# Summing a gradient over prompts on GpSimd in place of identity matmuls, with seven rotating PSUM banks

## The chip, the cores and the metric
The kernel runs on one core of one Trainium2 chip. The metric is the device time of one execution in microseconds. PE is the matrix engine (PEld its weight loads), DVE the vector engine, ACT the scalar engine, POOL the GpSimd engine, SP the engine whose queue issues many of the transfers. DVE, ACT and PE work with PSUM, the accumulator memory of eight banks; a bank holds 128 x 512 fp32 values.

## The reference
The forward pass is a speech encoder with a joint network; the kernel computes the output and all gradients (inputs bf16):

```python
B, T, D, K = 2, 16000, 256, 3      # U = 8 prompts
...
h = gelu(conv(x, w1))[:, ::2, :]   # 3 taps, every second step kept
f = gelu(conv(h, w2))[:, ::2, :]   # 4000 steps are left
fe = jnp.einsum("btd,de->bte", f, w_f)
ge = jnp.einsum("bud,de->bue", g, w_g)
j = jnp.tanh(fe[:, :, None, :] + ge[:, None, :, :])
return jnp.einsum("btud,dv->btuv", j, w_o)
```

`reference` returns this output and the gradients of `x`, `w1`, `w2`, `g`, `w_f`, `w_g` and `w_o` for a given `grad_out` of shape 2 x 4000 x 8 x 256. On the way back the gradient of the tanh's argument, (1 - j²) · (grad_out w_oᵀ), is summed over the eight prompts to give the gradient of `fe`. That sum is what the change is about. In the code it is kept with the opposite sign (NGZ, NGFE).

## The kernel before, in words
The 4000 steps of each of the two batches are cut into chunks of 512 (the last has 416): G = 16 chunks, numbered from 0. Channels lie on the partitions: a tile of 2 x 512 columns holds 256 channels of one chunk, and W is the chunk's width.

The main loop goes over chunks n, and in each over four pairs of prompts (`joint_units`, a generator that yields after each piece of work). For each prompt u of a pair, `gj` squares the tanh on ACT (JSQ), multiplies the transposed `grad_out` by w_oᵀ on PE into a PSUM tile (L518), and on DVE forms NGZ = (JSQ - 1) · that tile (L520), one tile half at a time. Then come the output blocks (`o_block`: PE L574, copied by ACT to OUT, L576), the sum over prompts (`ngfe_acc`), and the products for w_o's gradient (`gwo`, L621) of the pair before, for which the tanh is transposed by DMA (JR, L548). At the end of a pair its outputs are stored from POOL's queue (L605).

Into this main work a second stream is woven, `fill`: after each main unit `weave` takes 0.85 units of it on the average. For a chunk n in the middle it holds, in this order: `d1_units(n - 1)` (gradient through w_f; PE L334 reads NGFE, DVE writes GF, L336), `conv_units(n + 1)` (first convolution of the next chunk, four PSUM tiles, PE L241), `d5_units(n - 1)` (GH, L366), six units of `gw2_units(n - 1)` (PE transposes copied out by DVE, L374 and L376), `conv2_units(n + 1)` (L274), the rest of `gw2_units` (sums added up by DVE, L317), and `e_units(n - 1)` (gradients of x and w1: L467, L489), with `fe_units(n + 1)` (L297) among them. What is left of `fill` after the fourth pair runs then.

The gelu and its derivative are not instructions of these units: `gelu` puts ten operations a tile (nine on DVE, a sigmoid on ACT; their line is L191, where they are called) into a list `later`, of which `pump(2)` takes two before each fill step; `conv2_units` and `fe_units` empty it first. All work on bf16 tiles of 128 x 1024 in SBUF.

PSUM: a pool `psp` of five rotating banks for all short-lived tiles (`ps`, `pst`), one bank for `GWO_ps`, and `psn` for `NGps`, a tile of 128 x 2 x 512 fp32, which fills two. NGZ has three buffers, OUT and JSQ two, X5 four.

`load_x5` loads the rows of x for w1's gradient from POOL's queue, pinned to the program order. `d1_units` calls it when its first unit is taken. POOL further stores OUT and GX and copies halo columns of HT, G1, GF and GH (L232, L256, L328, L354).

Of the kernel before, what the change touches and what calls it, by code (L numbers as in the profile page):

```python
# [14 lines left out]
FP32 = mybir.dt.float32  # L15
ALU = mybir.AluOpType
# [5 lines left out]
P = 128  # L22
KT = 2
# [3 lines left out]
U = 8  # L27
CW = 512
# [3 lines left out]
def kernel(  # L32
# [22 lines left out]
    nc = tc.nc  # L55
# [7 lines left out]
    def geom(n):  # L63
        b, ci = chunks[n]
        c0 = ci * CW
        return b, ci, c0, min(CW, MQ - c0)

    def blocks(w):
        return [(o, min(P, w - o)) for o in range(0, w, P)]
# [7 lines left out]
    ftp = pool("ftp", 2)  # L77
    fep = pool("fep", 2)
    ngp = pool("ngp", 1)
    gfp = pool("gfp", 2)  # L80
    ghp = pool("ghp", 2)
    rowp = pool("rowp", 6)
# [7 lines left out]
    jrp = pool("jrp", 2)  # L90
    outp = pool("outp", 2)
    PS = bass.MemoryType.PSUM
    psp = pool("psp", 5, space=PS)
    psn = pool("psn", 1, space=PS)
    psw = pool("psw", 1, space=PS)

    def ps_f32():
# [6 lines left out]
    ident = const.tile([P, P], BF16, name="ident")  # L104
# [52 lines left out]
    def window(n):  # L157
        b, ci, c0, W = geom(n)
        lo = c0 - 1 if ci > 0 else 0
        hi = c0 + W if ci == NCH - 1 else c0 + W - 1  # L160
        return lo, hi

    def load_x5(n, o, M):
        pin = tc.keep_in_program_order
        b = chunks[n][0]
        q0 = window(n)[0] + o
        t = x5p.tile([P, 5, D], BF16, name="X5")
        if q0 == 0:
            nc.vector.memset(t[0:1, 0, :], 0.0)
            pin(nc.gpsimd.dma_start(out=t[0:1, 1:5, :], in_=x[b, 0:4, :].rearrange("(o f) d -> o f d", o=1)))  # L170
            src = x[b, 3:4, :]
            ap5 = bass.AP(tensor=src.tensor, offset=src.offset, ap=[[4 * D, M - 1], [1, 5 * D]])
            pin(nc.gpsimd.dma_start(out=t[1:M].rearrange("p f d -> p (f d)"), in_=ap5))
        else:
            src = x[b, 4 * q0 - 1:4 * q0, :]
            ap5 = bass.AP(tensor=src.tensor, offset=src.offset, ap=[[4 * D, M], [1, 5 * D]])
            pin(nc.gpsimd.dma_start(out=t[:M].rearrange("p f d -> p (f d)"), in_=ap5))
        S[n]["X5", o] = t
# [140 lines left out]
    def d1_units(n):  # L319
        b, ci, c0, W = geom(n)  # L320
        st = S[n]
        lo, hi = window(n)
        for (o, M) in blocks(hi - lo):
            load_x5(n, o, M)
        GF = gfp.tile([P, KT, CW + 4], BF16, name="GF")
        st["GF"] = GF
        if ci > 0:
            nc.gpsimd.tensor_copy(out=GF[:, :, 1:2], in_=S[n - 1]["GF"][:, :, CW + 1:CW + 2])  # L328
        if ci == NCH - 1:
            nc.gpsimd.memset(GF[:, :, 2 + W:3 + W], 0.0)  # L330
        for mt in range(KT):
            ps = ps_f32()
            for kt in range(KT):
                nc.tensor.matmul(ps[:, :W], lhsT=WFT[:, kt, mt * P:(mt + 1) * P], rhs=st["NGFE"][:, kt, :W],  # L334
                                 start=(kt == 0), stop=(kt == KT - 1))
            nc.vector.scalar_tensor_tensor(out=GF[:, mt, 2:2 + W], in0=st["G2"][:, mt, :W], scalar=-1.0,  # L336
                                           in1=ps[:, :W], op0=ALU.mult, op1=ALU.mult)
            yield
# [184 lines left out]
            yield  # L523

    def ngfe_acc(n, u):
        W = geom(n)[3]
        st = S[n]
        if u == 0:
            st["NGps"] = psn.tile([P, KT, CW], FP32, name="NGps")
        for mt in range(KT):  # L530
            nc.tensor.matmul(st["NGps"][:, mt, :W], lhsT=ident[:], rhs=st["NGZ", u][:, mt, :W],  # L531
                             start=(u == 0), stop=(u == U - 1))
        if u == U - 1:
            st["NGFE"] = ngp.tile([P, KT, CW], BF16, name="NGFE")
            nc.scalar.copy(out=st["NGFE"][:, :, :W], in_=st["NGps"][:, :, :W])

    def load_jr(n, up):

# [16 lines left out]
    def joint_units(n, up):  # L555
        b, ci, c0, W = geom(n)
        st = S[n]
        bl = blocks(W)
        us = (2 * up, 2 * up + 1)
        for u in us:  # L560
            yield from gj(n, u)
        if n == 0:
            for k in range(len(bl)):
                jr_block(n, up, k)
                yield
        OUT = outp.tile([P, 4, 2 * V], BF16, name="OUT")
        JR = st["JR", up]

        def o_block(k):
            o, M = bl[k]  # L570
            ps = ps_f32()
            for j, u in enumerate(us):
                for kt in range(KT):
                    nc.tensor.matmul(ps[:M, j * V:(j + 1) * V], lhsT=st["JT", u][:, kt, o:o + M], rhs=WO[:, kt, :],  # L574
                                     start=(kt == 0), stop=(kt == KT - 1))
            nc.scalar.copy(out=OUT[:M, k, :], in_=ps[:M, :])  # L576

        pend = prev_gwo[0]
        o_block(0)
        yield  # L580
        o_block(1)
        if len(bl) > W // P:
            jr_block(n, up, len(bl) - 1)
        yield
        ngfe_acc(n, us[0])
        if pend is not None:
            gwo(*pend, 0)
        yield
        if pend is not None:
            gwo(*pend, 1)  # L590
        yield
        for k in range(2, len(bl)):
            o_block(k)
            yield
            if pend is not None:
                gwo(*pend, k)
        ngfe_acc(n, us[1])
        yield
        if pend is not None:
            for k in range(len(bl), len(blocks(geom(pend[0])[3]))):  # L600
                gwo(*pend, k)
        yield
        prev_gwo[0] = (n, up)
        nfull = W // P
        nc.gpsimd.dma_start(out=out_0[b, c0:c0 + nfull * P, us[0]:us[1] + 1, :].rearrange("(tb p) u v -> p tb (u v)", p=P),  # L605
                            in_=OUT[:, 0:nfull, :])
        if W > nfull * P:
            nc.gpsimd.dma_start(out=out_0[b, c0 + nfull * P:c0 + W, us[0]:us[1] + 1, :].rearrange("t u v -> t (u v)"),
                                in_=OUT[:W - nfull * P, nfull, :])
# [3 lines left out]
    def gwo(n, up, k):  # L613
        bl = blocks(geom(n)[3])
        if k >= len(bl):
            return
        o, M = bl[k]
        JR, GO = S[n]["JR", up], S[n]["GO", up]
        for j in range(2):
            for dt in range(KT):  # L620
                nc.tensor.matmul(GWO_ps[:, dt, :], lhsT=JR[:M, k, j, dt, :], rhs=GO[:M, k, j * V:(j + 1) * V],  # L621
                                 start=(n_gwo[0] == 0), stop=(n_gwo[0] == last_gwo))
                n_gwo[0] += 1


    def chain(*gens):
        for gen in gens:
            yield from gen
# [81 lines left out]
    for n in range(G):  # L710
        back, fwd = n > 0, n + 1 < G
        parts = []
        if back:
            d1, d5, gw2, e = d1_units(n - 1), d5_units(n - 1), gw2_units(n - 1), e_units(n - 1)
        if back:
            parts.append(d1)
        if fwd:
            parts.append(conv_units(n + 1))
        if back:
            parts += [d5, islice(gw2, 6)]  # L720
        if fwd:
            parts.append(conv2_units(n + 1))
        if back:
            parts += [gw2, islice(e, 5)]
        if fwd:
            parts.append(fe_units(n + 1))
        if back:
            parts.append(e)
        fill = chain(*parts)
        ratio = (0.85 if n > 0 else 0.2) if n + 1 < G else 0.72  # L730
        for up in range(U // 2):
            step = n * (U // 2) + up
            for i in range(2):
                if 2 * step + 4 + i < len(order):
                    load_got(*order[2 * step + 4 + i])
            if step + 1 < len(orderp):
                load_go(*orderp[step + 1])
            if up == 2 and n + 2 < G:
                load_x(n + 2)
            main = joint_units(n, up)  # L740
            weave(main, fill, ratio)
            if up == U // 2 - 1:
                for _ in fill:
                    pump(2)
                pump(len(later))
            for i in range(2):
                if 2 * step + 2 + i < len(order):
                    tanh(*order[2 * step + 2 + i])
            if step + 1 < len(orderp):
                load_jr(*orderp[step + 1])  # L750
    n = G - 1
    for k in range(len(blocks(geom(n)[3]))):
        gwo(*prev_gwo[0], k)
    for _ in chain(d1_units(n), d5_units(n), gw2_units(n), e_units(n)):
        pass

# [72 lines left out]
```

## Time and profile before
| what | value |
|---|---|
| median of 3 runs | 951.14 us (947.83 to 953.77) |
| the profiled execution | 953.21 us, its span 951.4 us |
| granted PE clock, mean | 0.989 |
| DMA queues' packets, share of 16 engines | 64.3% (hardware), 25.2% (software) |
| NGZ on DVE (L520) | 256 instructions, mean 668 ns |
| NGFE copy on ACT (L535) | 16 instructions, median 1000 ns |

Busy times count each engine's own instructions. A wait in square brackets in a timeline is idle time of the engine just before the instruction, with what ended it. The chain of waits runs back from the last instruction, at each step to what released it. Matmuls overlap in the array, so that each one's record is longer than the time after which the next begins.

### The profile page before, as it was taken

What the parts mean: (1) busy time and instruction counts of PE and PEld (TensorE: products, weight loads), DVE (VectorE), ACT (ScalarE), POOL (GpSimd) and SP (SyncE); (2) the same over time, 40 slices, a digit from 0 to 9 for tenths busy, and PEclk for the clock granted to TensorE, in tenths of its full rate; (3) what the DMA queues carried; (4) which work ended last, traced back from release to release, by engine and by line L of the source; (5) the groups of instructions that cost most, each with busy time, mean ns of one, the idle gap of its engine ahead of it and who ended that gap; (6) DMA issues with size and microseconds to landing.
All of it is one profiled execution on the core that took longest, in us unless ns stands there. A gap on an engine that the chain in (4) does not pass through costs nothing.

```text
span 951.4 us, 18311 instructions
## 1 busy us (share of the span) xinstructions
PE 914.8 (96%) x6976; PEld 629.1 (66%) x6976; DVE 633.1 (67%) x1364; ACT 614.4 (65%) x972; POOL 144.8 (15%) x279
## 2 busy tenths in 40 slices
PE   7889998999999999999999999899999999999997
PEld 3455665767667576766756667576676757677775
DVE  5887847678494866748587494865939578494634
ACT  2878484765848567583865848568484866858433
POOL 1002121121111112021111202012021120202121
PEclk9989999999999999999999999999999999999999
DMA  9769999799998999898799999989989997897742
GB/s 189 175 125 221 194 207 204 198 230 186 212 196 206 206 203 244 183 219 187 156 211 192 200 206 209 198 190 221 205 208 228 188 226 179 191 215 183 198 132 87
DMA packets 381816, 185.69 MB, mean 195 GB/s; under 512 B 329904, under 2 KB 365512, under 8 KB 381728
## 3 DMA queue, kind: packets, MB, share of 16 engines
q1 hardware_dynamic: 362016, 114.35, 64.3%
q0 software_dynamic: 19712, 70.18, 25.2%
q8 instruction: 54, 0.88, 0.4%
q14 instruction: 34, 0.28, 0.1%
HBM read 54.43 MB, written 50.34 MB: 110 GB/s over the span
## 4 chain that ended last, share of the span: by engine, by line
PE 53%; DVE 24%; ACT 17%; DMA 4%; issue 2%; POOL 0%; SPq 0%; ACTq 0%; POOLq 0%; DVEq 0%
PE ps L489 8%; PE ps L467 7%; PE ps L574 7%; PE GWO_ps L621 6%; DVE g_sq L191 6%; DVE g_s L191 5%; ACT JT L307 5%; PE ps L518 5%; PE pst L374 5%; PE ps L274 4%; DVE NGZ L520 4%; DVE GH L366 4%; DMA JR<-JT 3%; ACT OUT L576 3%; PE NGps L531 2%; ACT JSQ L512 2%
## 5 line engine op out<-in xcount | busy, mean ns | idle before, releaser
L520 DVE SCALAR_TENSOR_TENSOR NGZ<-JSQ,ps 128x512 bf16<-128x512 bf16 (+1 forms) x256 | 167.7, 668 | 108.1 <-PE ps L518 102.9
L576 ACT CAST OUT<-ps 128x512 bf16<-128x512 f32 (+1 forms) x256 | 150.4, 591 | 81.7 <-PE ps L574 80.1
L307 ACT ACTIVATE JT<-FE,GE 128x512 bf16<-128x512 f32 (+1 forms) x256 | 172.8, 717 | 2.6 <-PE ps L574 2.0
L512 ACT ACTIVATE JSQ<-JT 128x1024 bf16<-128x1024 bf16 (+1 forms) x128 | 133.0, 1040 | 54.5 <-DVE NGZ L520 54.0
L621 PE MATMUL GWO_ps<-GO,JR 128*128 128x256 bf16 (+1 forms) x1024 | 153.1, 273 | 9.2 <-DMA JR<-JT 9.1
L574 PE MATMUL ps<-WO,JT 128*128 128x256 bf16 (+1 forms) x1024 | 156.0, 275 | 0.1
L518 PE MATMUL ps<-GOT,WOT 128*128 128x512 bf16 (+1 forms) x512 | 138.4, 374 | 6.3 <-DVE NGZ L520 5.9
L621 PEld LDWEIGHTS <-JR 128*128 128x128 bf16 (+1 forms) x1024 | 98.7, 97 | 50.2 <-DMA JR<-JT 14.0
L574 PEld LDWEIGHTS <-JT 128*128 128x128 bf16 (+1 forms) x1024 | 98.3, 99 | 32.1 <-issue 6.2
L317 DVE TENSOR_TENSOR ACC<-ACC,ps 128x512 f32<-128x512 f32 x90 | 61.4, 684 | 83.9 <-PE ps L489 80.4
L191 ACT ACTIVATE g_s<-g_s 128x1024 bf16<-128x1024 bf16 (+2 forms) x49 | 49.2, 1004 | 89.5 <-DVE g_s L191 89.5
L467 PE MATMUL ps<-W1T,GH 128*128 128x256 bf16 (+2 forms) x768 | 103.7, 272 | 0.0
L489 PE MATMUL ps<-rows,X 128*128 128x256 bf16 (+2 forms) x768 | 93.6, 272 | 0.0
L470 ACT CAST GX<-ps 128x512 bf16<-128x512 f32 (+2 forms) x128 | 75.3, 588 | 28.3 <-PE ps L467 19.4
L241 PE MATMUL ps<-XC,W 128*128 128x512 bf16 (+1 forms) x384 | 91.0, 374 | 0.7 <-DVE JR L376 0.5
L467 PEld LDWEIGHTS <-GH 128*128 128x128 bf16 (+2 forms) x768 | 74.7, 99 | 20.6 <-issue 1.6
L605 POOL DMA_DIRECT2D out_dram<-OUT x64 | 49.1, 767 | 247.5 <-ACT OUT L576 244.1
L376 DVE COPY rows<-pst 128x1024 bf16<-128x1024 bf16 (+5 forms) x134 | 85.8, 655 | 1.4 <-PE pst L374 1.4
L479 POOL DMA_DIRECT2D out_dram<-GX x64 | 35.3, 552 | 321.1 <-ACT GX L470 315.7
L489 PEld LDWEIGHTS <-X 128*128 128x128 bf16 (+2 forms) x768 | 73.7, 97 | 14.8 <-issue 3.0
L531 PE MATMUL NGps<-NGZ,ident 128*128 128x512 bf16 (+1 forms) x256 | 80.3, 374 | 0.1
L191 DVE TENSOR_TENSOR g_sq<-g_x 128x1024 bf16<-128x1024 bf16 (+2 forms) x49 | 32.1, 655 | 68.1 <-ACT g_x L244 39.3
(122 smaller groups left out, 1156.7 us busy)
## 6 DMA issues: line engine op xcount, KB each, us to landing
GO<-in_grad_out_dram SPq DMA_DIRECT2D x56, 512.0 KB, 4.2
out_dram<-OUT POOLq DMA_DIRECT2D x56, 512.0 KB, 4.8
X<-in_x_dram POOLq DMA_DIRECT2D x58, 320.0 KB, 7.6
out_dram<-GX POOLq DMA_DIRECT2D x58, 256.0 KB, 3.0
JR<-JT SPq DMA_TRANSPOSE x240, 3.7
GO<-in_grad_out_dram SPq DMA_DIRECT2D x8, 384.0 KB, 3.9
out_dram<-OUT POOLq DMA_DIRECT2D x8, 384.0 KB, 4.1
GOT<-in_grad_out_dram SPq DMA_TRANSPOSE x128, 4.9
```

The costliest lines, as they stand in the source:

```text
L191: later.popleft()()
L241: nc.tensor.matmul(ps[:, :W], lhsT=W1[:, i, kt, mt * P:(mt + 1) * P], rhs=st["X", c][:, kt, 16 + sh:16 + sh + W], start=(k == 0), stop=(k ...
L307: nc.scalar.activation(out=JT[:, mt, :W], in_=S[n]["FE"][:, mt, :W], func=ACT.Tanh, bias=GE[:, b, mt, u:u + 1], scale=1.0)
L467: nc.tensor.matmul(ps[:Mx, cj * D:(cj + 1) * D], lhsT=GH[:, par, kt, j:j + Mx], rhs=W1T[:, i, kt, :], start=(k == 0), stop=(k == last))
L489: nc.tensor.matmul(ps[:, dt * D:(dt + 1) * D], lhsT=st["X5", o][:M, i + 2 * par, dt * P:(dt + 1) * P], rhs=t[:M, j + 2 * par:j + 2 * par + ...
L512: nc.scalar.activation(out=JSQ[:, :, :W], in_=JT[:, :, :W], func=ACT.Square)
L518: nc.tensor.matmul(ps[:, :W], lhsT=WOT[:, kt, mt * P:(mt + 1) * P], rhs=GOT[:, kt, :W], start=(kt == 0), stop=(kt == KT - 1))
L520: nc.vector.scalar_tensor_tensor(out=NGZ[:, mt, :W], in0=JSQ[:, mt, :W], scalar=1.0, in1=ps[:, :W], op0=ALU.subtract, op1=ALU.mult, accum_ ...
L531: nc.tensor.matmul(st["NGps"][:, mt, :W], lhsT=ident[:], rhs=st["NGZ", u][:, mt, :W], start=(u == 0), stop=(u == U - 1))
L574: nc.tensor.matmul(ps[:M, j * V:(j + 1) * V], lhsT=st["JT", u][:, kt, o:o + M], rhs=WO[:, kt, :], start=(kt == 0), stop=(kt == KT - 1))
L576: nc.scalar.copy(out=OUT[:M, k, :], in_=ps[:M, :])
L621: nc.tensor.matmul(GWO_ps[:, dt, :], lhsT=JR[:M, k, j, dt, :], rhs=GO[:M, k, j * V:(j + 1) * V], start=(n_gwo[0] == 0), stop=(n_gwo[0] == ...
```

## The change
The sum over prompts moves from PE to POOL. Before, two identity matmuls a prompt added NGZ to `NGps` in PSUM, and after the eighth ACT copied it as bf16 to NGFE. Now the sum is kept in SBUF (`ACCN`, fp32): from the second prompt on POOL adds NGZ to it in one instruction of 128 x 1024 (the second adds the first two tiles), and the eighth writes NGFE as bf16. The call comes right after `gj` of the prompt, ahead of the output blocks; it came after the second output block for a pair's first prompt, and after the last for its second. The two banks of `NGps` go to `psp`. `d1_units` moves behind `conv_units` in the fill, and `load_x5` out of it, ahead of the chunk's first pair.

```diff
+    accp = pool("accp", 1)
...
-    psp = pool("psp", 5, space=PS)
-    psn = pool("psn", 1, space=PS)
+    psp = pool("psp", 7, space=PS)
...
     def d1_units(n):
...
-        lo, hi = window(n)
-        for (o, M) in blocks(hi - lo):
-            load_x5(n, o, M)
...
     def ngfe_acc(n, u):
         W = geom(n)[3]
         st = S[n]
         if u == 0:
-            st["NGps"] = psn.tile([P, KT, CW], FP32, name="NGps")
-        for mt in range(KT):
-            nc.tensor.matmul(st["NGps"][:, mt, :W], lhsT=ident[:], rhs=st["NGZ", u][:, mt, :W],
-                             start=(u == 0), stop=(u == U - 1))
+            return
+        if u == 1:
+            st["ACCN"] = accp.tile([P, KT, CW], FP32, name="ACCN")
+        acc = st["ACCN"][:, :, :W]
+        in0 = st["NGZ", 0][:, :, :W] if u == 1 else acc
+        out = acc
         if u == U - 1:
             st["NGFE"] = ngp.tile([P, KT, CW], BF16, name="NGFE")
-            nc.scalar.copy(out=st["NGFE"][:, :, :W], in_=st["NGps"][:, :, :W])
+            out = st["NGFE"][:, :, :W]
+        nc.gpsimd.tensor_tensor(out=out, in0=in0, in1=st["NGZ", u][:, :, :W], op=ALU.add)
...
         for u in us:
             yield from gj(n, u)
+            ngfe_acc(n, u)
...
-        ngfe_acc(n, us[0])
...
-        ngfe_acc(n, us[1])
...
         if back:
-            parts.append(d1)
+            for (o, M) in blocks(window(n - 1)[1] - window(n - 1)[0]):
+                load_x5(n - 1, o, M)
         if fwd:
             parts.append(conv_units(n + 1))
         if back:
-            parts += [d5, islice(gw2, 6)]
+            parts += [d1, d5, islice(gw2, 6)]
...
+    for (o, M) in blocks(window(n)[1] - window(n)[0]):
+        load_x5(n, o, M)
     for _ in chain(d1_units(n), d5_units(n), gw2_units(n), e_units(n)):
```

## The prediction
> **What bounds the kernel now.** I read the page first, then the busy time of one steady chunk in five stretches, then that chunk's chain of waits and the timelines of DVE, PE and POOL in it.
>
> ```profile
> span 951.4 us, 18311 instructions
> PE 914.8 (96%) x6976; PEld 629.1 (66%) x6976; DVE 633.1 (67%) x1364; ACT 614.4 (65%) x972; POOL 144.8 (15%) x279
> PE 53%; DVE 24%; ACT 17%; DMA 4%; issue 2%; POOL 0%; SPq 0%; ACTq 0%; POOLq 0%; DVEq 0%
> L531 PE MATMUL NGps<-NGZ,ident 128*128 128x512 bf16 (+1 forms) x256 | 80.3, 374 | 0.1
> ```
>
> PE is busy for 96% of the span, yet the chain that ended last lies on DVE and ACT for 41% of it. So there are stages with different limits. Chunk 4, counted from 0, with its fill (250 to 307.9 us) shows them; the columns are stretch, length, then busy time and instruction count of PE, PEld, DVE, ACT, POOL, then clock, DMA share and GB/s:
>
> ```profile
> 250.00:263.70 13.70, 13.61 (x78) 7.43 (x77) 9.80 (x20) 10.03 (x16) 3.16 (x7) 1.00 1.08 242
> 263.70:276.30 12.60, 11.03 (x101) 7.67 (x100) 12.58 (x27) 4.92 (x7) 0.92 (x3) 1.00 1.03 165
> 276.30:278.50 2.20, 2.20 (x17) 1.39 (x15) 0.00 (x0) 1.56 (x3) 0.77 (x1) 1.00 0.69 153
> 278.50:290.00 11.50, 11.44 (x100) 8.74 (x98) 11.26 (x23) 5.68 (x8) 0.56 (x1) 1.00 1.03 219
> 290.00:307.90 17.90, 17.83 (x142) 13.72 (x141) 5.83 (x14) 16.76 (x29) 3.17 (x5) 1.00 0.87 203
> ```
>
> In two stretches, together 24.1 of 57.9 us, DVE never rests (12.58 of 12.6, 11.26 of 11.5): the gelu of the next chunk lies there. In the other three PE is full, and in the last ACT nearly so. On PE's side the DVE-full stretches show as waits for a PSUM bank:
>
> ```profile
> 266.64 0.59 PE L518 MATMUL ps<-GOT,WOT 128*128 128x512 bf16 x2 [0.59 <-DVE NGZ L520]
> 274.52 0.28 PE L621 MATMUL GWO_ps<-GO,JR 128*128 128x256 bf16 x1 [0.97 <-DMA JR<-JT]
> ```
>
> **What is removed.** The chain of this chunk prices a pair of identity matmuls by what it holds back:
>
> ```profile
> 283.73 0.43 PE NGps L531 x2
> 291.83 0.43 PE NGps L531 x2
> ```
>
> That is 0.43 us a pair; the page's 80.3 us is larger because records of pipelined matmuls overlap. 112 full pairs give 48.2 us, 16 pairs of 416 columns about 0.35 each (0.43 times 416/512), 5.6 us: 54 us of PE in all, 3.4 us a full chunk. What of it counts is read stretch by stretch. Three of the eight pairs (those that start at 267.07, 271.31 and 283.57) lie where DVE sets the pace; there PE would only wait longer, so I take nothing. Five lie where PE does: 2.15 us. The NGFE copy (16 x 1.0 us of ACT) goes too; PE waited 0.25 us for it ahead of the first d1 matmul at 250.59, so I take 0.25 us more. Together 2.4 us a steady chunk.
>
> **What is added.** 112 adds of 128x1024 on POOL, seven a chunk, fp32 sum plus bf16 gradient. No row shows such an add. Below lies a DVE row with two SBUF inputs: g_s on L191, the scalar_tensor_tensor, mean 1220 ns for the same 1024 elements. For the price on POOL I look at how POOL shares SBUF with DVE, since the small halo copies show it:
>
> ```profile
> 253.32 0.19 POOL L328 COPY GF<-GF 128x2 bf16<-128x2 bf16 x1 [1.12 <-DVE GF L336]
> 265.51 0.52 POOL L354 COPY GH<-GH 128x2 bf16<-128x2 bf16 x1 [2.54 <-DVE GH L366]
> 270.88 0.19 POOL L232 COPY HT<-HT 128x2 bf16<-128x2 bf16 x1 [4.85 <-DVE g_x L191]
> ```
>
> All three move two elements. The first and third run beside DVE instructions that take one operand from PSUM (NGZ, rows) and need 0.19 us. The second starts inside `HT<-g_s,g_x` (265.30 to 265.98, both inputs in SBUF) and ends 0.05 us after it: it was shut out for the rest of that instruction. Eleven of the 14 GH copies ran beside such an instruction and took 518 to 603 ns; the three that did not took 193 to 207. So there is one way into SBUF that POOL has and DVE uses for a second operand, and it is held for a whole instruction. An engine with one way reads two operands in two passes: 2 x 1.22 = 2.44, plus the 0.19 us of the smallest copy, 2.63 us, an estimate. Bounds: one pass, 1.22 + 0.19 = 1.4 us; three passes (the result written separately), 3.85 us. I take 2.63, since the copies speak for a single way in.
>
> By the Trainium skill (GPSIMD Engine Reference, Performance versus the Vector engine) a 2048-element fp32 add takes 4.5 us there, so 2.25 us here by estimate; no row shows it, and the sum would come to a tie, 944 us.
>
> POOL has room: 112 x 2.63 = 295 us beside its 145. What is shut out counts. The two-input and four-fold DVE instructions are the gelu's, 459 instructions with 282 us. They fill the very stretches in which DVE never rests, and four of a chunk's adds become ready there (prompts 2 to 5, NGZ finished at 267.8, 272.1, 283.1, 287.4):
>
> ```profile
> 267.71 0.69 DVE L191 TENSOR_TENSOR g_sq<-g_sq,HT 128x1024 bf16<-128x1024 bf16 x1
> 268.32 0.68 DVE L376 COPY rows<-pst 128x1024 bf16<-128x1024 bf16 x1
> 268.92 0.68 DVE L191 TENSOR_TENSOR G<-g_sq,g_s 128x1024 bf16<-128x1024 bf16 x1
> 269.52 0.68 DVE L520 SCALAR_TENSOR_TENSOR NGZ<-JSQ,ps 128x512 bf16<-128x512 bf16 x1
> ```
>
> The add of prompt 2 would wait out the first of these, run beside the second (0.60 us, from PSUM) and hold the third; the NGZ queued behind that on DVE, though it needs only PSUM and one SBUF operand, waits too, and PE behind it for the bank. So an add costs DVE 2.63 - 0.60 = 2.0 us; the order after the other three is the same. That an add shuts DVE out as DVE shuts POOL out isn't shown, only the mirror of it.
>
> The Trainium skill states it both ways (SBUF — State Buffer, Who interferes with whom): whichever instruction starts first holds the shared pair, and the other is blocked, not slowed.
>
> **What the two banks give.** In the first DVE-full stretch DVE empties nine banks from 265.90 to 275.01, one in 1.1 us; in the second ten from 279.11 to 289.08, the same. Two more banks let PE run 2.3 and 2.2 us further ahead. So PE loses 2 x 2.0 - 2.3 = 1.7 us in the first. The 2.2 us pause between (DVE waits for conv2's copy on ACT) is used up: DVE ends 4.0 late and conv2 comes 1.7 late. In the second PE loses 4.0 - 2.2 = 1.8. Together 3.5 us against 2.4 saved: +1.1 us a steady chunk.
>
> **Edits at nothing.** The X5 loads (4 x 0.54 us on POOL) were issued at 250.07, right behind the last store, and stay there; used some 30 us later (first gw1 at 288.7). Were they behind an add, they would land 2.6 us later, still covered. d1 behind conv: conv comes 1.7 us (250.59 to 252.3) earlier, GF's two DVE instructions (1.2 us) move into the full stretch, and the add of prompt 1 (ready at 253.8, or earlier) holds the first gelu instruction for up to 2 us of the 2.6 us that DVE idles now; I call it even. Behind a waiting add on POOL stand halo copies, OUT and GX stores: HT's copy is done 3.8 us before conv2 (270.88, 274.64), the two OUT buffers leave over ten us. NGZ has three buffers and prompts come 7 us apart, so an add of 2.6 us frees them in time.
>
> **Sum.** The profiled execution took 953.2 us (span 951.4 and 1.8 around it), 2.1 above the median of 951.14. Fourteen steady chunks: +15. The last chunk has no gelu, all eight pairs count, -3.4; chunk 0 even. 953.2 + 15 - 3.4 = 965 us.
>
> **Rivals.**
> Faster: PE's relief wins, because an add is near 1.4 us or DVE is shut out for only part of it. Then an add costs DVE up to 0.8 us and two of them (1.6) fit into the two banks: 14 x 2.4 + 3.4 = 37 less, 916 us. If the bank wait shown above (0.6 us) and the inner three pairs (1.3 us) come out too, 14 x 4.3 + 3.4 = 64 less, 889. It decides where an add costs DVE less than half of the two banks' lead, 1.1 us. For it: PE full in three stretches. Against it: the GH copies, and DVE's two full stretches. The DMA share (mean 0.98 here, highest 1.13 in any 20 us) leaves it room.
> Tie: an add of 2.3 us costs DVE 1.7 and PE 2 x (3.4 - 2.2) = 2.4 a chunk, just what is saved; the last chunk's 3.4 stay, 950 us (942 to 960).
> Much slower: three passes, 3.85 us. DVE loses 3.25 an add, PE 6.5 - 2.3 and 6.5 - 2.2, that is 8.5 - 2.4 = 6.1 a chunk: +82, 1035 us.
>
> **How the numbers follow.** Forecast (slower, 961 to 995) 0.40; faster 0.34; tie 0.16; much slower 0.10. Within 1% (9.5 us) is what a measurement of this kernel can't tell from no change. Faster 0.34; same 0.16, the tie; slower 0.50, the forecast and much slower. The range leaves out much slower and the deep end of faster: 905 to 1005.
>
> **What would show it.** Right: adds near 2.6 us; in the DVE-full stretches gelu instructions stretched to two or three times their 0.68 us, or gaps before them, while NGZ keeps 0.68; DVE-full stretches some 4 us longer each; the last stretch about 1 us shorter. Wrong: gelu rows unchanged beside adds, or PE's waits for banks gone, with chunks of 54 us; or adds at 3.5 us and POOL never idle.

## The result and the profile after

The changed kernel takes 1003.13 us (median of four runs, 999.01 to 1006.56) against 949.94 us before: a ratio of 1.055, 95% interval 1.050 to 1.061. It is slower, as forecast, and lies just inside the range's upper end of 1005 us; but the loss is 53 us where the sum gave 12. Ratios leave out executions in a slower state; among the kernels below only a_dve_late_x has any (911.0 and 912.6 us, against 897.3 and 901.3).

The page of the changed kernel (span; busy time by engine; shares of the chain that ended last; the group of the new adds):

```profile
span 1000.7 us, 17973 instructions
PE 882.4 (88%) x6720; PEld 609.2 (61%) x6720; DVE 718.5 (72%) x1364; ACT 593.2 (59%) x956; POOL 391.5 (39%) x391
DVE 35%; PE 27%; ACT 22%; issue 8%; DMA 4%; SPq 2%; POOL 1%; ACTq 0%; POOLq 0%; DVEq 0%
L536 POOL TENSOR_TENSOR ACCN<-ACCN,NGZ 128x1024 f32<-128x1024 f32 (+1 forms) x80 | 175.8, 2198 | 163.5 <-DVE NGZ L517 163.3
```

PE's share of the chain fell from 53% to 27%. DVE has the same number of instructions as before and is busy 85 us longer. Chunk 4 in its five stretches (262.2 to 321.6 us; the columns as in the prediction):

```profile
262.20:267.70 5.50, 5.50 (x29) 2.68 (x28) 2.70 (x8) 5.50 (x11) 4.25 (x7) 1.00 0.84 205
267.70:291.40 23.70, 19.39 (x156) 12.86 (x154) 22.79 (x38) 11.59 (x19) 7.95 (x8) 1.00 1.00 224
291.40:293.00 1.60, 1.60 (x13) 1.04 (x12) 0.00 (x0) 0.93 (x2) 0.77 (x1) 1.00 1.25 263
293.00:307.00 14.00, 11.33 (x100) 8.91 (x98) 13.94 (x23) 5.70 (x9) 5.10 (x3) 1.00 0.85 181
307.00:321.60 14.60, 14.56 (x119) 11.63 (x119) 4.67 (x11) 13.27 (x24) 6.08 (x5) 1.00 0.66 164
```

PE idles 4.3 us in the second and 2.7 us in the fourth, the stretches in which DVE sets the pace; the fourth is 2.5 us longer than before (14.0 against 11.5; about 4 us were forecast), the last 3.3 us shorter (1 us was forecast). The first two can't be compared one by one, since d1 now lies in the second. The chunk begins 12.2 us later than in the kernel before and ends 13.7 us later (262.2 against 250, 321.6 against 307.9); of the 49.3 us by which the span grew, the eleven chunks after it bring 35.6, some 3.2 each. So the loss is spread over all chunks, and this one has less than its share. How an add meets the gelu shows in the timelines of POOL and DVE:

```profile
297.77 2.18 POOL L536 TENSOR_TENSOR ACCN<-ACCN,NGZ 128x1024 f32<-128x1024 f32 x1 [4.94 <-DVE NGZ L517]
```

```profile
297.87 0.68 DVE L317 TENSOR_TENSOR ACC<-ACC,ps 128x512 f32<-128x512 f32 x1
298.47 2.03 DVE L191 TENSOR_TENSOR FT<-g_s,g_x 128x1024 bf16<-128x1024 bf16 x1
300.42 0.67 DVE L517 SCALAR_TENSOR_TENSOR NGZ<-JSQ,ps 128x512 bf16<-128x512 bf16 x1
```

The add runs from 297.77 to 299.95. Beside it the addition of L317, with one operand from PSUM, takes its usual 0.68 us. FT reads two operands from SBUF, comes in at 298.47 and ends at 300.50, 0.55 us after the add: 2.03 us in place of 0.68. Of the 112 adds 60 have a gelu instruction stretched in this way beside them, 2.02 us on the average. Five of the 60 are TENSOR_SCALARs, which read one operand only and take 0.42 us by themselves. The 19 NGZ instructions that lie wholly within an add take 0.67 us.

Where PE waits, first in the kernel before, then in the changed one (who waited for whom; total us, times, longest):

```profile
PE GWO_ps L621 <- DMA JR<-JT: 9.1, 11, 1.9
PE ps L518 <- DVE NGZ L520: 5.9, 10, 0.6
```

```profile
PE ps L360 <- DVE GF L333: 31.3, 27, 3.0
PE ps L486 <- DVE rows L373: 22.5, 25, 1.3
PE GWO_ps L621 <- DMA JR<-JT: 20.8, 23, 2.9
PE ps L464 <- DVE NGZ L517: 7.6, 11, 0.7
PE ps L576 <- DVE NGZ L517: 6.4, 8, 1.2
```

The largest waits are not for banks but for data: d5 for GF, the w1 gradient for its transposed rows, gwo for the transposed tanh JR. All three lie in SBUF, where PE reads them. So the question was what the adds cost, what d1's new place costs, and what the banks are worth.

### The profile page after: what moved, and what is told of

It reads as the page before. It is cut to its first block, busy times and chain, and to the rows that moved or that the text cites. A ratio compares the mean times of both kernels' runs of the same rounds, so it can differ in the third digit from the quotient of the medians.

```text
span 1000.7 us, 17973 instructions
## 1 busy us (share of the span) xinstructions
PE 882.4 (88%) x6720; PEld 609.2 (61%) x6720; DVE 718.5 (72%) x1364; ACT 593.2 (59%) x956; POOL 391.5 (39%) x391
## 4 chain that ended last, share of the span: by engine, by line
DVE 35%; PE 27%; ACT 22%; issue 8%; DMA 4%; SPq 2%; POOL 1%; ACTq 0%; POOLq 0%; DVEq 0%
DVE g_sq L191 11%; ACT JT L307 8%; DVE NGZ L517 5%; ACT JSQ L509 5%; PE ps L274 5%; DVE g_s L191 4%; PE GWO_ps L621 4%; PE ps L576 4%; PE ps L486 3%; DMA JR<-JT 3%; DVE G L191 3%; ACT GX L467 3%; ACT OUT L578 3%; DVE FT L191 3%; PE ps L360 2%
## 5 line engine op out<-in xcount | busy, mean ns | idle before, releaser
L536 POOL TENSOR_TENSOR ACCN<-ACCN,NGZ 128x1024 f32<-128x1024 f32 (+1 forms) x80 | 175.8, 2198 | 163.5 <-DVE NGZ L517 163.3
L307 ACT ACTIVATE JT<-FE,GE 128x512 bf16<-128x512 f32 (+1 forms) x256 | 175.6, 740 | 23.6 <-PE ps L576 22.0
L621 PE MATMUL GWO_ps<-GO,JR 128*128 128x256 bf16 (+1 forms) x1024 | 156.1, 279 | 22.7 <-DMA JR<-JT 20.8
L576 PE MATMUL ps<-WO,JT 128*128 128x256 bf16 (+1 forms) x1024 | 160.7, 278 | 9.5 <-DVE NGZ L517 6.4
L509 ACT ACTIVATE JSQ<-JT 128x1024 bf16<-128x1024 bf16 (+1 forms) x128 | 135.3, 1059 | 21.4 <-DVE NGZ L517 21.3
L317 DVE TENSOR_TENSOR ACC<-ACC,ps 128x512 f32<-128x512 f32 x90 | 61.6, 685 | 79.6 <-PE ps L486 76.5
L191 DVE TENSOR_TENSOR g_sq<-g_x 128x1024 bf16<-128x1024 bf16 (+2 forms) x49 | 49.0, 1000 | 52.5 <-ACT g_x L277 40.3
L360 PE MATMUL ps<-GF,W2T 128*128 128x512 bf16 (+2 forms) x192 | 56.5, 407 | 32.5 <-DVE GF L333 31.3
```

The source lines that it names most:

```text
L191: later.popleft()()
L307: nc.scalar.activation(out=JT[:, mt, :W], in_=S[n]["FE"][:, mt, :W], func=ACT.Tanh, bias=GE[:, b, mt, u:u + 1], scale=1.0)
L509: nc.scalar.activation(out=JSQ[:, :, :W], in_=JT[:, :, :W], func=ACT.Square)
L536: nc.gpsimd.tensor_tensor(out=out, in0=in0, in1=st["NGZ", u][:, :, :W], op=ALU.add)
```

## The experiments

Times are medians; the ratio is to runs of the kernel before on the same chip, with its 95% interval. Those runs had medians of 948.9 to 953.7 us. Differences in the text are between medians; worked out from the ratios they are up to 8 us larger or smaller, which is said where it matters.

### The changed kernel, taken apart

**a_d1_first**

```diff
+        if back:
+            parts.append(d1)
         if fwd:
             parts.append(conv_units(n + 1))
         if back:
-            parts += [d1, d5, islice(gw2, 6)]
+            parts += [d5, islice(gw2, 6)]
```

> The changed kernel with d1_units back in front of conv_units; adds on POOL and seven banks stay. Theory A (two causes: adds shut DVE out, and d1 right ahead of d5 leaves GF's latency bare, 2.1 + 0.3 us of PE wait a chunk): the wait before L360 goes, 14 x 2.4 = 33 us less than the changed kernel, some 970 us. Rival B (the order is harmless, the lost DVE time comes out somewhere else in the same stretch): 995 to 1005 us, with the wait before L360 turned into bank waits before L515 and L371.

966.6 us, 1.015 (1.011 to 1.020). 36.5 us are gone, about what theory A said, and the wait for GF with them. But PE's wait for JR's transposes (20.8 us in the changed kernel) is gone too, so that this run alone doesn't show that GF was the cause. The adds were as they are (gelu 365 us in all, against 282 before and 366 in the changed kernel). What the prediction called even cost two thirds of the loss.

**b_d1_late**: the same order in the kernel before.

```diff
-        lo, hi = window(n)
-        for (o, M) in blocks(hi - lo):
-            load_x5(n, o, M)
...
-        if back:
-            parts.append(d1)
+        if back:
+            for (o, M) in blocks(window(n - 1)[1] - window(n - 1)[0]):
+                load_x5(n - 1, o, M)
...
-            parts += [d5, islice(gw2, 6)]
+            parts += [d1, d5, islice(gw2, 6)]
...
+    for (o, M) in blocks(window(n)[1] - window(n)[0]):
+        load_x5(n, o, M)
```

> The kernel before with one edit alone: d1_units behind conv_units and the X5 loads ahead of the first pair; identity matmuls and five banks stay, no add on POOL. Theory A: a PE wait for GF ahead of d5 appears also without the adds, but shorter, since DVE is less behind: 0.5 to 1.5 us a chunk, 958 to 972 us. Rival B: 947 to 955 us.

1037.3 us, 1.089 (1.084 to 1.094). Both expectations missed, by far: without a single add on POOL this one edit costs some 84 us. And it isn't GF that PE waits for most:

```profile
PEld L618 <- DMA JR<-JT: 76.0, 43, 5.8
PE GWO_ps L618 <- DMA JR<-JT: 64.2, 39, 5.5
PE ps L360 <- DVE GF L333: 8.0, 14, 0.8
```

PE waits 64 us for JR (the second column of names tells who is waited for; PEld is the weight load of the same matmul) and 8 us for GF. So theory A was wrong in what d1's place does here. Nor are waits all of the cost: PE is busy for 941.1 us, against 914.8 in the kernel before, with the same 6976 matmuls. PE's idle time grew by 58 us, its busy time by 26.

**b_hoist** has the moved X5 loads of b_d1_late and d1 in front, so that only the loads differ from before.

> The kernel before with the X5 loads issued ahead of the chunk's first pair, and nothing else; d1_units stays in front. If the cost of b_d1_late (84 us) comes from d1 behind conv: the time of before, 945 to 960 us. If moving the loads costs it: above 1000 us.

951.4 us, 1.003 (0.999 to 1.007). Moving the loads costs nothing, as the prediction said.

**a_one_add** leaves out the sum over prompts 0 to 5; the lines of `ngfe_acc` that make ACCN, ahead of the ones shown, are gone too.

```diff
...
         if u == U - 1:
             st["NGFE"] = ngp.tile([P, KT, CW], BF16, name="NGFE")
-            out = st["NGFE"][:, :, :W]
-        nc.gpsimd.tensor_tensor(out=out, in0=in0, in1=st["NGZ", u][:, :, :W], op=ALU.add)
+            nc.gpsimd.tensor_tensor(out=st["NGFE"][:, :, :W], in0=st["NGZ", u - 1][:, :, :W],
+                                    in1=st["NGZ", u][:, :, :W], op=ALU.add)
```

> The changed kernel with one add of the seven left, the last, which adds the gradients of prompts 6 and 7; the sum over prompts 0 to 5 is left out. PE's relief, the seven banks and the new order stay. Theory A (adds shut DVE out: 84 us of longer gelu instructions): gelu instructions back at 0.68 us, PE waits for GF 0.5 to 1.5 us a chunk, PE's relief counts: 905 to 930 us. Rival C (PE was not what could be won, the transfers or ACT bound the kernel once PE has 54 us less): 940 us or more.

970.9 us, 1.019 (1.014 to 1.024). The gelu is back at 283 us, but the time fits rival C: PE waits 47 us for JR here and 15 us for GF. Taken by itself this run would have said that the adds cost 32 us, and that PE's relief is worth nothing.

**a_one_add_d1_first** is a_one_add with d1 in front.

> The changed kernel with d1_units in front again and one add of the seven left (prompts 6 and 7; the sum over prompts 0 to 5 is left out). Against a_d1_first (966.6 us) only the adds are missing. Theory A (84 us of longer gelu instructions hold PE back): 905 to 925 us, PE's relief of some 40 us against the kernel before is seen in full. Rival C (without the adds something else holds, as in a_one_add, where PE waited 61 us for JR): 935 us or more.

905.9 us, 0.950 (0.943 to 0.957): theory A. Against a_d1_first the six adds a chunk cost 61 us; against the kernel before, PE's relief and the banks are worth 43 us (48 by the ratios).

**a_5banks** changes `psp = pool("psp", 7, space=PS)` to 5.

> The changed kernel with five rotating banks in place of seven, two left unused. If the two banks hide 2.2 us of DVE's lag in each of two stretches a chunk, as the prediction had it: 14 x 4.4 = 62 us more, up to 1065 us. If PE waits for data (GF, rows, JR) more than for banks: under 15 us more, 1003 to 1018 us.

1085.8 us, 1.142 (1.135 to 1.148), 83 us more, above what even the prediction's count of 62 us gave. But the largest new wait is JR again, 81 us in place of 21.

**a_d1_first_5b** is a_d1_first with five banks.

> a_d1_first (966.6 us) with five rotating banks in place of seven. The prediction gave the two banks 2.2 us in each of two stretches a chunk, 14 x 4.4 = 62 us: some 1028 us. If the 83 us of a_5banks came from d1's new place, as in b_d1_late, and banks themselves give little: 967 to 990 us.

1057.9 us, 1.113 (1.109 to 1.117): 91 us more than with seven. This rules out that the 83 us were only d1's place. The page of waits of this kernel:

```profile
PE GWO_ps L621 <- DMA JR<-JT: 79.2, 47, 6.5
```

### Why JR is late

JR is the tanh of a pair, transposed by four DMAs from SP's queue. In b_d1_late SP's queue and PE look so around one such wait:

```profile
283.63 8.45 SPq L135 DMA_TRANSPOSE XC<-in_x_dram  x3
292.19 5.15 SPq L545 DMA_TRANSPOSE JR<-JT  x4
```

```profile
288.97 0.49 PE L618 MATMUL GWO_ps<-GO,JR 128*128 128x256 bf16 x3
294.65 0.39 PE L618 MATMUL GWO_ps<-GO,JR 128*128 128x256 bf16 x1 [5.20 <-DMA JR<-JT]
294.84 1.06 PE L571 MATMUL ps<-WO,JT 128*128 128x256 bf16 x4
```

Three loads of x for a later chunk's convolution (XC) stand ahead of JR in SP's queue and keep it for 8.45 us; JR is issued at 292.19. On PE, gwo stands ahead of the output block that comes next (L571, which needs only JT). Both orders are made when the kernel is built: the program calls for XC in the chunk's third pair and for gwo between output blocks, but the builder may place an instruction earlier in its engine's queue. XC stood ahead of JR in the kernel before, too:

```profile
263.71 6.91 SPq L135 DMA_TRANSPOSE XC<-in_x_dram  x3
270.72 5.16 SPq L548 DMA_TRANSPOSE JR<-JT  x4
```

There SP came to JR 2.8 us before PE needed it (at 273.55; the wait of 0.97 us that the prediction shows ends at 274.52). In b_d1_late it comes to JR 2.7 us after that (292.19 against 289.45). Why d1's move shifts the two against each other by 5.6 us was not followed further.

The lost time has a second part. These are the 18 us ahead of JR's wait and the 20 us around it, columns as before, the granted clock third from the end:

```profile
262.00:280.00 18.00, 17.80 (x120) 11.52 (x119) 8.93 (x19) 16.38 (x28) 3.97 (x7) 1.00 0.85 199
280.00:300.00 20.00, 12.41 (x85) 7.46 (x85) 13.04 (x26) 4.35 (x6) 2.01 (x3) 0.80 0.98 167
```

The granted clock falls from 1.00 to 0.80, and the four matmuls of L571 behind the wait take 1.06 us, where four others took 0.60 us at 278.10. Over the whole kernel the mean clock is 0.954 in b_d1_late, 0.989 in the kernel before, and 0.993 and 0.997 in the next two runs, in which JR's waits are all but gone. The 26 us of longer busy time go with it: in those two PE is busy for 910.6 and 906.5 us.

The next two runs undo one of the two orders each.

**b_d1_late_pin**

```diff
-                nc.tensor.matmul(GWO_ps[:, dt, :], lhsT=JR[:M, k, j, dt, :], rhs=GO[:M, k, j * V:(j + 1) * V],
-                                 start=(n_gwo[0] == 0), stop=(n_gwo[0] == last_gwo))
+                m = nc.tensor.matmul(GWO_ps[:, dt, :], lhsT=JR[:M, k, j, dt, :], rhs=GO[:M, k, j * V:(j + 1) * V],
+                                     start=(n_gwo[0] == 0), stop=(n_gwo[0] == last_gwo))
+                tc.keep_in_program_order(m)
```

> b_d1_late (1037 us) with the gwo matmuls kept in program order on PE, nothing else. In b_d1_late they stand ahead of output blocks and transposes on PE, and PE waits 5 to 6 us a chunk there for the JR transposes. Theory F (d1's new place costs by the order in which PE's queue is laid out: gwo pulled ahead of work that could cover its data): 955 to 985 us. Rival G (the data are late whatever the order: JR lands late, GF is late): 1015 us or more, with the wait at another instruction.

958.7 us, 1.010 (1.005 to 1.015): theory F. 79 of the 84 us go with the order on PE alone.

**b_d1_late_x**

```diff
-                nc.sync.dma_start_transpose(out=t[:, :, 0:W + 16], in_=xq[b, c, c0 - 16:c0 + W, :])
+                tc.keep_in_program_order(nc.sync.dma_start_transpose(out=t[:, :, 0:W + 16], in_=xq[b, c, c0 - 16:c0 + W, :]))
...
-                nc.sync.dma_start_transpose(out=t[:, :, 16:16 + W], in_=xq[b, c, c0:c0 + W, :])
+                tc.keep_in_program_order(nc.sync.dma_start_transpose(out=t[:, :, 16:16 + W], in_=xq[b, c, c0:c0 + W, :]))
```

> b_d1_late with the loads of x for the convolution (XC, DMA transposes) kept in program order on SP's queue, so that they do not stand ahead of the pair's JR transposes (8.5 us of SP in b_d1_late). Theory H (JR lands late because XC goes first in SP's queue): the waits for JR go, 960 to 990 us. Rival F (PE's order): JR earlier helps in part, 990 to 1040 us; XC later may hold conv instead.

943.1 us, 0.990 (0.987 to 0.993), below what either theory gave, and 1% below the kernel before. SP's queue in the same part of the chunk:

```profile
265.57 5.13 SPq L545 DMA_TRANSPOSE JR<-JT  x4
270.76 0.57 SPq L149 DMA_DIRECT2D GO<-in_grad_out_dram  x1
271.38 5.05 SPq L135 DMA_TRANSPOSE XC<-in_x_dram  x2
```

JR now goes first, and PE's wait for it is 1.9 us in all. So either order undone removes the cost: it takes a late JR and a gwo that is placed early to lose the time. The chain is shown for the kernel before with d1 moved; the same edit on SP's queue was then made to the others.

**b_x**: the kernel before with that edit.

> The kernel before with the XC loads kept in program order on SP, d1 in front. Before waits 9 us at gwo for JR. Theory H: those go and little else, 938 to 948 us, so that d1 behind conv (b_d1_late_x, 943 us) costs nothing by itself. Rival: below 930 us, and d1's place costs 13 us or more even so.

939.0 us, 0.986 (0.980 to 0.991). The kernel before lost 12 us there too. With SP's queue mended, d1 behind conv costs 4 us at most (943.1 against 939.0; the intervals overlap).

**a_x**: the changed kernel with that edit.

> The changed kernel (1003 us) with the XC loads kept in program order on SP's queue, behind the pair's JR transposes. Theory H (d1's place costs through JR behind XC): the 33 us of waits at gwo go and the GF wait before L360 shrinks or is made up elsewhere, 955 to 975 us. Rival A (GF's latency behind a DVE held up by adds is what costs): the GF wait of 2 to 3 us a chunk stays, 980 to 1000 us.

972.7 us, 1.015 (1.007 to 1.023): 30 us of the changed kernel's time were JR's (38 by the ratios). The GF wait did not shrink, though, as theory H had let it:

```profile
PE ps L360 <- DVE GF L333: 31.4, 25, 3.0
PE ps L486 <- DVE rows L373: 22.6, 25, 1.3
```

**a_d1_first_x**: a_d1_first with it.

> a_d1_first (966.6 us), which waits only 4 us at gwo, with the XC loads kept in program order. Theory H: nothing to mend, 958 to 970 us. Were it much faster, the adds would not be what is left between it and a_one_add_d1_first (906 us).

965.7 us, 1.012 (1.009 to 1.015), as a_d1_first. In the mended queue d1's place costs 7 us beside the adds (3 by the ratios): the 31 us that PE waits for GF are for the most part waits that come elsewhere when d1 stands in front.

**a_d1_first_5b_x**: the five banks with it.

> a_d1_first with five banks (1058 us, of which PE waits 100 us at gwo for JR), with the XC loads kept in program order. Theory H: the waits at gwo go, 965 to 1000 us, and the banks by themselves are worth under 35 us. Rival (bank waits as the prediction counted them, 62 us): 1015 us or more.

973.5 us, 1.018 (1.011 to 1.025). Two banks are worth 8 us (5 by the ratios), not 62 and not 91. JR's wait, in place of 79.2:

```profile
PE GWO_ps L621 <- DMA JR<-JT: 12.9, 22, 1.7
```

**a_one_add_x**: a_one_add with it.

> a_one_add (971 us, of which PE waits 61 us for JR; the sum over prompts 0 to 5 is left out) with the XC loads kept in program order. Theory H with the adds at 61 us: 972.7 - 61 = 912, 903 to 920 us. If the adds cost less where d1 stands behind conv: 920 to 945 us.

893.9 us, 0.940 (0.935 to 0.945), faster than either theory's figure. Against a_x the adds cost 79 us (71 by the ratios) with d1 behind conv; they cost 61 us with d1 in front. That is more than the GF wait explains by itself (13.8 us are left of it here, of 31.4), and the division of the rest is open.

### The sum elsewhere

**a_pool_late**

```diff
-    jsp = pool("jsp", 2)
-    ngzp = pool("ngzp", 3)
+    jsp = pool("jsp", 5)
...
-        NGZ = ngzp.tile([P, KT, CW], BF16, name="NGZ")
+        NGZ = JSQ
...
         for u in us:
+            if u == U - 2:
+                later.extend(partial(ngfe_acc, n, v) for v in range(2, u))
             yield from gj(n, u)
-            ngfe_acc(n, u)
+            if u < 2:
+                ngfe_acc(n, u)
+            if u >= U - 2:
+                later.append(partial(ngfe_acc, n, u))
```

In place of adding each prompt's gradient as it is finished, the adds from the third prompt on are put off until the chunk's last pair.

> a_d1_first with the adds of prompts 2 to 7 put off to the chunk's last pair, two a main unit, where no gelu runs; NGZ is written over JSQ in one pool of five buffers so that the tiles can wait (3 + 2 buffers before). Theory A (it is the meeting with the gelu that costs): gelu instructions at 0.68 us, 905 to 930 us. Rival D (POOL is too slow in the last pair: six adds of 2.2 us, 13 us, in a stretch of some 15, hold NGFE and the NGZ buffers back): PE waits for NGFE at the chunk's start and ACT for JSQ's buffers, 945 to 980 us.

974.4 us, 1.023 (1.018 to 1.028): rival D, and more than that. Six adds do not fit in the last pair, and what is left over meets the next chunk's gelu, which stays at 363 us; ACT waited 33 us for the buffers that POOL's adds held.

**a_dve_late**: the same with `nc.vector.tensor_tensor`.

> The same as a_pool_late with all seven adds on DVE, no POOL arithmetic at all. An add of 128x1024 with fp32 operands on DVE some 1.2 us (g_s, the slow gelu instruction, 1.22 us): 8.4 us a chunk, in the last stretch, where DVE rests 12 of 17.9 us. Theory A: 905 to 930 us, near a_one_add_d1_first. Rival E (adds in DVE's queue hold NGZ and the bank behind them): 940 us or more.

923.8 us, 0.970 (0.966 to 0.975), theory A. One query of the trace by tile (duration in ns: least, median, most; first and last start):

```profile
L535 DVE TENSOR_TENSOR ACCN<-ACCN,JSQ x80: 1003/1219/1227, 55.3 to 883.1; 128x1024 f32<-128x1024 f32 x70, 128x832 f32<-128x832 f32 x10
```

The add takes 1.22 us on DVE, 2.2 us on POOL, and with it on DVE no two-operand gelu instruction of 1024 elements takes more than 0.70 us.

**a_dve_late_pin**: a_dve_late with gwo kept in order on PE.

> a_dve_late (923.8 us, PE waits 28.8 us for JR ahead of gwo) with the gwo matmuls kept in program order on PE. Theory F: those waits go and are partly found as other waits, 905 to 918 us. Rival G: 918 to 930 us.

921.3 us, 0.969 (0.965 to 0.972): rival G. The waits for JR went, and others of the same size came (PE for rows, 12 us in place of 1).

**a_dve_late_x**: a_dve_late with XC kept in order on SP.

> a_dve_late (923.8 us, 28.8 us of waits at gwo) with the XC loads kept in program order on SP. Theory H: 895 to 915 us. Rival: DVE and ACT bound it, 915 to 925 us.

906.2 us, 0.939 (0.930 to 0.949). It is the fastest kernel here that computes all of it: PE's 54 us are taken off, the sum runs where DVE rests, and JR comes in time.

## Why the prediction was right and wrong

The account, in the four runs with SP's queue mended: before 950.7; queue mended 939.0 (-12); PE's relief, seven banks, the new order and one add 893.9 (-45); the other adds 972.7 (+79); the queue as it was 1003.1 (+30). Each step starts where the one before ends, so the sum of +52 has to come near the +53 measured; and the sizes hold for this order alone. Without the adds the queue costs 77 us (970.9 against 893.9), with them 30 to 38. In the prediction's own terms, with the queue as it was: PE's relief and the banks -43 (-37 was forecast for the relief), the adds +61 (+49), d1's place +36.5 (0).

- **What is removed.** 37 us were taken as counting (2.4 a chunk and 3.4 in the last), 54 at the most. Measured together with the banks: 43 to 45. That fits.
- **The price of an add.** 2.63 us was the estimate from two passes over the slow DVE row and a smallest copy; 2.2 us was measured (medians 2.12 to 2.17). The estimate from the Trainium skill (GPSIMD Engine Reference, Performance versus the Vector engine), 2.25 us, was nearer; by it the sum would have been the tie, further from the result. (By the prediction's own terms that tie is 946 us, not 944.)
- **That an add shuts out DVE's two-input instructions.** Right, and now shown from the side that was missing: 2.01 us against 0.68 in 55 cases, NGZ untouched. The Trainium skill (SBUF — State Buffer, Who interferes with whom) has it so, and this trace agrees. An add that was met cost DVE 1.4 us, not 2.0; 84 us of DVE time in all, where 8.0 a chunk made 112.
- **What that costs PE.** 3.5 us a chunk, 49 us, was the sum; 61 us was measured with d1 in front and 79 us behind conv. The term was too small although its DVE part was too large, and what fits is that the 62 us set against it for the banks were too much: 84 less the 8 us measured is 76, an estimate. The path from DVE to PE was taken to be the banks alone, but in the changed kernel PE waits 54 us for data that DVE makes, GF and the transposed rows; with two banks fewer (a_5banks) these waits are 41 us, not longer.
- **The two banks.** 2.2 to 2.3 us in each stretch, 62 us, was wrong in kind: 5 to 8 us with SP's queue mended. The rest of the 91 us without is JR's.
- **"d1 behind conv ... I call it even".** This is the step that failed worst: 36.5 us in the changed kernel, 84 us in the kernel before. In its place the runs showed late JR: with XC out of its way 30 of the 36.5 us go, and of the 84 at most 4 stay (943.1 against 939.0). The prediction weighed conv's lead, GF's two instructions and the add of prompt 1 on DVE, and not what else a moved step moves: when PE comes to gwo, and when SP comes to JR behind XC. The trace of before showed a sign of it, quoted in the prediction and left unread: PE's 0.97 us wait for JR at 274.52, with JR right behind XC's 6.9 us on SP.
- **X5 loads at nothing.** Right (b_hoist).
- **The much slower rival** named three passes, 3.85 us an add, as its cause. Its time was nearer than the forecast's, its cause was not there.

That the order with d1 in front would have come out at 967, two from the forecast's 965, is chance: an add that was too dear and banks that were too good stood against each other.

## What to carry to other kernels

Moving a step in the program moves its neighbours in every queue; before calling that free, list for each queue what stood between a transfer and its user, above all where the profile already shows a short wait for it. Such a wait can cost more than its length: here a third of b_d1_late's loss was matmuls that took longer at a lower clock. An extra buffer covers only waits for buffers: count data waits by themselves. An idle engine that shares a way into memory with a full one isn't idle capacity; here the full engine's own resting stretch was the better place, once the sum was put off until then.

## What the runs showed of the hardware

A POOL add of 128x1024 takes nearly the same whether it reads bf16 and bf16 (median 2118 ns), fp32 and bf16 (2170) or writes bf16 (2118). On DVE the same add takes 1219 ns. A gelu instruction with two SBUF operands that meets a POOL add ends 0.55 us after it in the timeline above, nearly its own length of 0.68: as if it ran whole once the add was over. The 54 two-operand instructions that were stretched after beginning within an add ended 0.55 us after it in the median. One operand can be enough: the five TENSOR_SCALARs that began within an add took 1.87 to 2.31 us in place of 0.37 to 0.42 and ended 0.23 to 0.29 us after it. The add itself took 2.18 us, against 2.13 for the add at 289.06 us beside which DVE only ran copies from PSUM: it was hardly slowed.

Behind long waits of PE the granted clock was lower: 0.80 over the 20 us around a wait of 5.20 us in b_d1_late, 1.00 over the 18 us ahead of it.
